# Loading the second quarter of the pole tables four rounds earlier, with PSUM split three and two instead of two and four in the first nine rounds

## Chip, cores and metric

The kernel runs on one core of a Trainium2 chip. The metric is the device time of one execution in microseconds (us); the time of a kernel is the median of several runs.

## What is computed

One transformer-like block on 2048 tokens of width 576. A modulation vector (`silu(c) @ w_mod`) gives six rows of 576. Part A is a layer norm, a modulation and a long convolution whose kernel comes from complex poles; part B is a layer norm, a modulation and a gated MLP whose gate mixes the tokens with a 2048x2048 matrix.

```python
mod = (silu(c) @ w_mod).reshape(1, 6, 1, -1)            # sa, ca, ga, sb, cb, gb
h = layernorm(x) * (1 + ca) + sa
K = einsum("dn,dnl,dn->dl", C, exp(dt*A*l), dt*B).real  # 576 channels, 128 poles, 2048 taps
x = x + ga * (irfft(rfft(h) * rfft(K)) + h * Dskip)
h = layernorm(x) * (1 + cb) + sb
z = gelu(h @ w_in); z1, z2 = halves(z)
x = x + gb * ((z1 * (w_sp @ layernorm(z2) + b_sp)) @ w_out)
```

## The kernel before

The change lies in part A, the function `ssm`. It works in **rounds** (the loop `for tick in range(NG + 4)`, L703; the first round is tick 0, so the fourth is tick 3). The 576 channels make 36 **groups** of 16, numbered g. Each round starts one group, and each group passes through a chain of steps, one round or so apart:

- `e_unit(g)` (L444), for three groups at a time in every third round: three matmuls of the table `lb` with a selector. Two fill a two-bank PSUM tile (`ps`, L450), one fills a one-bank tile (`pk`, L453). ScalarE takes the exponential of both (L451, L454).
- `t_unit(g)` (L458): matmuls of the tables `lc` and `la` (L467, L471) put the phases into a two-bank tile. For the first ten groups VectorE copies them out (L479); from group 10 on ScalarE and VectorE round them (L482, L483). L484 takes the absolute value.
- `s_unit(g)` (L487): two ScalarE sines, a cosine (L489) and a sine (L490).
- `p_unit(g)` (L492): four VectorE products (L500 to L503).
- `kg_unit(g)` (L506): 32 small matmuls into a one-bank tile (L513); ScalarE copies it to `kab` (L516), and VectorE adds the skip (L520).
- `k1_unit(g)` (L522): 8 matmuls into a one-bank tile (L530), copied out by ScalarE (L537) or VectorE (L535).

Beside this chain runs the input. In rounds 0 to 7 `ln_pair` (L423) transforms two of the 16 row blocks of x, in two halves: each half takes two two-bank tiles at once, fills them with 16 matmuls that the trace shows as 8 in bf16 and 16 in f32 (L433), and ScalarE copies each tile out (L435). The program calls a round's work LN(j) below. GpSimd then stores the block to `u_d` (L436). The row blocks come in four loads `ln_x` (L380) into two buffers, each with its statistics on VectorE (L408 to L410). In rounds 3 to 5 `mod_unit` (L342) makes one more row of the modulation: a matmul of `wm` (L349), a copy (L351), a second matmul (L354), a copy (L369 or L371) and a store by GpSimd (L372). From round 9 on `u_load`, `u_unit`, `z_unit` and `v_unit` (L572 to L603) take `u_d` through the convolution, beginning with `u_unit` (L580, L581) in round 10.

The tables `lb`, `lc` and `la` hold a quarter of the channels, nine groups, each. `poles` (L199) makes them on VectorE and ScalarE and writes them to DRAM (`pa_d`, `pb_d`) through GpSimd's queue; for the last three quarters that ends in round 2. `poles_load` (L296) brings one quarter back: a memset and six transfers of 48x1152 bf16, all issued by GpSimd in program order. Each table has two buffers. Quarter 0 is loaded ahead of the rounds, quarter 1 in round 7, quarter 2 in round 13, quarter 3 in round 21 (L787). Group 9 is the first that reads quarter 1.

PSUM has eight banks of 512 floats per partition. Through the whole of `ssm` they are two `ps` tiles of two banks and four `pk` tiles of one (L174, L182 to L186). At the start of round 9 `early.close()` (L705) ends the pools that only the input needs.

The order within an engine's queue is the program's only where the call goes through `tied` (`Pin`, L142). Most calls of the rounds don't: a scheduler sets their order when the program is built, and the wait for a PSUM tile is one of the things that it goes by. Part B is tied throughout.

Of the kernel before, what the change touches and what calls it, by code (L numbers as in the profile page):

```python
# [9 lines left out]
F32 = mybir.dt.float32  # L10
# [5 lines left out]
PSUM = bass.MemoryType.PSUM  # L16
# [148 lines left out]
def ssm(tc, I, x1_d, consts_s, dram, mod_d, mlp):  # L165
# [5 lines left out]
    with ExitStack() as ctx:  # L171
        cp = ctx.enter_context(tc.tile_pool(name="cp", reuse_waits="tile", bufs=1, side="right"))
        kp = ctx.enter_context(tc.tile_pool(name="kp", reuse_waits="tile", bufs=2, side="right"))
        psp = ctx.enter_context(tc.tile_pool(name="psp", bufs=2, space=PSUM, reuse_waits="tile"))  # L174
        early = ctx.enter_context(ExitStack())

        u1_d = dram.tile([4, 16, 2, 32, D], F32, name="u1_d")
        v_d = [dram.tile([128, 32, w], F32, name="v_d") for w in CHW]
# [1 line left out]
        pb_d = dram.tile([4, 2, 6, CW // 2], BF, name="pb_d")  # L180

        def ps2():  # L182
            return psp.tile([128, 2, 512], F32, name="ps")

        def ps1():
            return psp.tile([128, 512], F32, name="pk", bufs=4)  # L186

        mlp.ps1 = ps1
        small = cp.tile([128, 6, 128], F32, name="small")
# [106 lines left out]
        def poles_load(c, Q):  # L296
            for n, d_, k in (("lb", pb_d, 0), ("lc", pa_d, 0), ("la", pa_d, 3)):
                t_ = tb.tile([112, 9, 128], BF, name=n)
                if n == "lb":
                    Q.memset(t_[32:64], 0.0)  # L300
                for h in range(2):
                    Q.dma_start(t_[64 * h:64 * h + 48], d_[c, h, k:k + 6].rearrange("q (c g n) -> (q c) g n", c=8, g=9))
                lt[n, c] = t_
# [22 lines left out]
        def mod_load(k):  # L326

            if k < 2:
                t = kp.tile([128, 32, 128], F32, name="k1").rearrange("p a b -> p (a b)")
                wmt[k] = [t[:96, 6 * HC * hh:6 * HC * hh + 6 * HC].rearrange("p (k n) -> p k n", k=6) for hh in range(2)]  # L330
            else:
                wmt[k] = [ep.tile([96, 6, HC], F32, name="wm") for hh in range(2)]
            for hh in range(2):
                S.dma_start(wmt[k][hh], I["w_mod"][:, k, hh])
# [7 lines left out]
        def mod_unit(k):  # L342
            wm = wmt.pop(k)
            mpart = ep.tile([128, D], F32, name="mpart", bufs=1)
            pm = ps2()
            for hh in range(2):
                for kt in range(6):
                    j = kt % 4
                    T.matmul(pm[32 * j:32 * j + 32, hh, :HC], ec[:, kt:kt + 1].to_broadcast([96, 32]),  # L349
                             wm[hh][:, kt], start=kt < 4, stop=kt >= 2, skip_group_check=True)  # L350
            A.activation(v3(mpart), pm[:, :, :HC], AF.Copy)  # L351
            pm = ps2()
            for hh in range(2):
                T.matmul(pm[:, hh, :HC], ones, mpart[:, HC * hh:HC * hh + HC], start=True, stop=True)  # L354
            src = pm[:, :, :HC]
            if k == 2:
                A.activation(v3(gar), src, AF.Copy)
            elif k == 1:
                V.scalar_tensor_tensor(v3(cga), src, 1.0, v3(gar), op0=ALU.add, op1=ALU.mult)
            elif k == 0:  # L360
                V.tensor_tensor(v3(sga), src, v3(gar), op=ALU.mult)
                for i in range(2):
                    A.activation(gsp, sga, AF.Copy)
                    V.scalar_tensor_tensor(sga, gsp, msk[:, i:i + 1], sga, op0=ALU.mult, op1=ALU.add)
                A.activation(gsp, sga, AF.Copy)
            else:
                mrow = ep.tile([128, D], F32, name="gar", bufs=1)
                if k == 4:
                    A.activation(v3(mrow), src, AF.Identity, bias=one)  # L369
                else:  # L370
                    A.activation(v3(mrow), src, AF.Copy)  # L371
                G.dma_start(mod_d[k - 3:k - 2], mrow[0:1])  # L372
# [5 lines left out]
        def ln_load(i):  # L378
            x4s[i] = ep.tile([128, 4, D], F32, name="ln_x")
            S.dma_start(x4s[i], I["x"][:, 4 * i:4 * i + 4])  # L380

        def r1_load(i):
            r1t[i] = ep.tile([128, 2, 2, 32], F32, name="r1t"), ep.tile([128, 2, 2, 32], BF, name="cs")
            S.dma_start(r1t[i][0], I["c_r1t"][:, 2 * i:2 * i + 2])
            S.dma_start(r1t[i][1], I["c_cs"][:, 2 * i:2 * i + 2])
# [58 lines left out]
        def e_unit(g):  # L444
            c, gi = divmod(g, 9)
            lb = lt["lb", c]
            e = et[g] = tb.tile([128, 1536], F32, name="et", bufs=5)
            pa = ps2()
            for h, (l, r) in enumerate(zip(halves(lb, gi), rows(256, 512))):
                T.matmul(pa[:, h], l, r, start=True, stop=True)  # L450
            A.activation(e[:, :1024].rearrange("p (h n) -> p h n", h=2), pa, AF.Exp)  # L451
            pb = ps1()
            T.matmul(pb, lb[:, gi], sel[:, 1024:1536], start=True, stop=True)  # L453
            A.activation(e[:, 1024:], pb, AF.Exp)  # L454
# [113 lines left out]
        def cst_load(kg):  # L568
            cst[kg] = cs.tile([128, 8, 128], F32, name="cst%d" % kg)
            S.dma_start(cst[kg], I["c_st"][:, 8 * kg:8 * kg + 8])  # L570
# [132 lines left out]
        for tick in range(NG + 4):  # L703
            if tick == 9:
                early.close()  # L705
                cs = ctx.enter_context(tc.tile_pool(name="cs", reuse_waits="tile", bufs=1, side="right"))
                sb = ctx.enter_context(tc.tile_pool(name="sb", reuse_waits="tile", bufs=2, side="right"))
                wpre = ctx.enter_context(tc.tile_pool(name="wpre", reuse_waits="tile", bufs=2, side="right"))
            if 9 <= tick < 13:
                cst_load(tick - 9)  # L710
            if tick == 16:
                st4 = cs.tile([128, 16, 2, 64], F32, name="st4")
                S.dma_start(st4, I["c_st4"])
            if tick in (20, 24):
                mlp.start_load(tick // 4 - 5, wpre)
            todo = plan.get(tick, [])

            def go(fn):
                for f, a in todo:
                    if f is fn:  # L720
                        f(*a)

            def lag(fn, n):
                if 0 <= tick - n < NG:
                    fn(tick - n)

            if tick == 0:
                for g in range(3):
                    e_unit(g)
            go(y_load)  # L730
            go(u_load)
            es = iter(range(tick, tick + 3) if tick % 3 == 0 and 0 < tick < NG else ())

            def e_one():
                for g in es:
                    e_unit(g)
                    break

            if tick < 10:
                go(z_unit)  # L740
                lag(p_unit, 2)
                lag(t_unit, 0)
                lag(s_unit, 1)
                go(v_unit)
                lag(kg_unit, 3)
                go(u_unit)
                lag(k1_unit, 4)
                go(y_unit)
                lag(d_unit, 3)
                if tick == 0:  # L750
                    T = nc.tensor
                for _ in range(3):
                    e_one()
            else:
                go(z_unit)
                lag(p_unit, 2)
                lag(t_unit, 0)
                lag(s_unit, 1)
                lag(kg_unit, 3)
                lag(k1_unit, 4)  # L760
                go(y_unit)
                go(v_unit)
                e_one()
                go(u_unit)
                lag(d_unit, 3)
                e_one()
                e_one()
            if tick < 5:
                next(p1, None)
                next(p1, None)  # L770
            if tick == 0:
                mod_load(3)
            if 3 <= tick < 6:
                mod_unit(tick)
                if tick < 5:
                    mod_load(tick + 1)
            j = tick
            if j < 8:
                if j in (2, 4):
                    ln_stats(j // 2 + 1)  # L780
                ln_pair(2 * j)
                if j < 6:
                    r1_load(j + 2)
                if j in (1, 3):
                    ln_load(j // 2 + 2)
            if tick in (7, 13, 21):
                poles_load(1 + (tick > 7) + (tick > 13), mlp.tied.gpsimd)  # L787


        tabs.close()  # L790
# [1429 lines left out]
```

## Time and profile before

| what | us |
|---|---|
| median of 3 runs (1778.59 to 1780.67) | 1779.78 |
| the profiled execution's own time | 1784.37 |
| its span, first to last instruction | 1782.6 |
| TensorE busy, VectorE busy, ScalarE busy, GpSimd busy | 1669.4, 1259.5, 832.1, 244.5 |
| part A, rounds 3 to 9, by the copies L479 of groups 3 to 9 | 92.25 to 173.20 |
| part A, rounds 10 to 35, by L483 of groups 10 to 35 | 176.9 to 365.2 |

Times in the views are from the span's start. PE is TensorE (its matmuls), PEld its weight loads, DVE is VectorE, ACT ScalarE, POOL GpSimd, SP the queue that issues most loads. "x" stands ahead of a count. In a timeline a row has the start, the length, the engine, the line, the operation, the tile written and the tile read, and in brackets how long the engine had been idle and what ended that. L152 is a helper's line and stands for any tied call. A granted clock (PEclk) of 1.00 is TensorE's full speed.

### The profile page before, as it was taken

To read this page: it belongs to the slowest core of one execution; us is meant where nothing else is said; L and a number is where in the kernel's file an instruction comes from. 1 tells how busy PE (TensorE), PEld (TensorE's weight loads), DVE (VectorE), ACT (ScalarE), POOL (GpSimd) and SP (SyncE) were. 2 spreads that over 40 slices of the span, in tenths; PEclk is the share of its full clock that TensorE was granted. 3 is DMA by queue.
4 is the path that set the end of the run, shared out by engine and by line. 5 is a ranking of instruction groups with operands and counts; after the bars stand their busy time and mean duration, and the time that the engine had idled before them with its cause. 6 is when DMAs were issued, how large, how long until landed. Compare 5 with 4: busy or idle time off the path is not lost.

```text
span 1782.6 us, 36406 instructions
## 1 busy us (share of the span) xinstructions
PE 1669.4 (94%) x15174; PEld 1247.6 (70%) x15174; DVE 1259.5 (71%) x2259; ACT 832.1 (47%) x1118; POOL 244.5 (14%) x400
## 2 busy tenths in 40 slices
PE   3687899997899999999989999999999999999999
PEld 1243556665455445777878888888888888888887
DVE  6874899966898998688899677688344478344432
ACT  4766998844567656445434444234222223122210
POOL 3322232333122211000000000000111100111100
PEclk9587999998999999999999999999999999999999
DMA  9466646679688779767665886873767573556531
GB/s 259 134 178 184 188 121 181 184 216 294 205 255 259 248 230 266 285 245 251 233 222 165 278 302 244 269 247 124 250 219 231 195 235 98 192 195 217 193 111 40
DMA packets 183381, 376.24 MB, mean 211 GB/s; under 512 B 39360, under 2 KB 103488, under 8 KB 182448
## 3 DMA queue, kind: packets, MB, share of 16 engines
q1 hardware_dynamic: 140416, 175.23, 32.5%
q0 software_dynamic: 36896, 172.01, 29.3%
q10 hardware_dynamic: 5904, 26.67, 3.7%
q8 instruction: 119, 1.95, 0.5%
q14 instruction: 46, 0.38, 0.1%
HBM read 263.11 MB, written 101.31 MB: 204 GB/s over the span
## 4 chain that ended last, share of the span: by engine, by line
PE 65%; DVE 14%; DMA 7%; ACT 5%; issue 5%; POOL 2%; SPq 1%; ACTq 0%; DVEq 0%; POOLq 0%
PE ps L152 53%; PE pz L152 2%; DVE zset L152 2%; PE pk L513 2%; DVE bsz L152 2%; PE pk L530 2%; DMA wsst<-in_w_spT 1%; PE pk L592 1%; DVE gt L152 1%; DMA ln_x<-in_x 1%; DMA zset<-set_d 1%; PE pk L600 1%; DVE wsp L152 1%; DVE n L152 1%; DVE rq L152 1%
## 5 line engine op out<-in xcount | busy, mean ns | idle before, releaser
L152 PEld LDWEIGHTS <-zset 128*128 128x128 f16 x7182 | 702.7, 98 | 92.8 <-DVE zset L152 8.1
L152 PE MATMUL ps<-wsp,zset 128*128 128x256 f16 x6048 | 668.9, 273 | 7.1 <-DVE zset L152 6.5
L152 PE MATMUL pz<-wz,nt 128*128 128x512 f16 (+1 forms) x1120 | 224.1, 360 | 12.9 <-ACT nt L152 5.9
L152 PEld LDWEIGHTS <-nt 128*128 128x128 f16 x1120 | 109.5, 99 | 121.3 <-ACT nt L152 7.5
L152 ACT ACTIVATE z<-gt 128x1024 f16<-128x1024 f32 x56 | 59.0, 1054 | 289.6 <-DVE gt L152 289.6
L152 DVE SCALAR_TENSOR_TENSOR gt<-ps,sc,bsp 128x512 f32<-128x512 f32 x36 | 27.0, 749 | 205.0 <-PE ps L152 203.3
L1928 POOL DMA_DIRECT2D zset<-set_d x96 | 50.8, 530 | 869.7 <-PE ps L152 616.3
L152 PE MATMUL ps<-wout,z 128*128 128x288 f16 x1344 | 170.0, 286 | 0.0
L152 PEld LDWEIGHTS <-z 128*128 128x128 f16 x1344 | 131.5, 98 | 33.0
L152 DVE TENSOR_TENSOR raw<-raw 128x512 f32<-128x512 f32 (+2 forms) x228 | 119.1, 528 | 13.6 <-DMA raw<-z_d 9.3
L152 PE MATMUL ps<-n2o,zset 128*128 128x256 f16 x1134 | 128.2, 273 | 0.0
L152 DVE SCALAR_TENSOR_TENSOR gt<-ps,sc,gt 128x512 f32<-128x512 f32 (+1 forms) x180 | 122.2, 696 | 7.6
L152 DVE TENSOR_TENSOR zset<-raw,zset 128x1792 f16<-128x1792 f32 x48 | 96.9, 2019 | 14.3 <-ACT zset L152 14.3
L152 ACT ACTIVATE zset<-raw 128x1792 f16<-128x1792 f32 x48 | 81.1, 1690 | 54.7 <-PE ps L152 22.2
L152 DVE TENSOR_TENSOR z<-ps,z 128x512 f32<-128x512 f32 (+1 forms) x126 | 71.9, 598 | 36.8 <-ACT z L152 25.0
L152 ACT ACTIVATE wsp<-raw,sc 128x1792 f16<-128x1792 f32 x25 | 44.6, 1784 | 42.7 <-DVE raw L152 35.0
L152 ACT ACTIVATE z<-z,sc 128x1024 f32<-128x1024 f32 x21 | 24.1, 1148 | 75.6 <-DVE z L152 71.9
L152 ACT ACTIVATE z<-pz,sc 128x512 f32<-128x512 f32 (+1 forms) x96 | 51.7, 581 | 13.1 <-PE pz L152 7.1
L152 ACT ACTIVATE z<-z,nm,r 128x1152 f32<-128x1152 f32 x24 | 31.5, 1342 | 52.0 <-DVE nm L152 30.7
L152 PE MATMUL ps<-n2q,wf 128*128 128x512 f16 x252 | 55.7, 379 | 0.0
L501 DVE TENSOR_TENSOR pg<-et,ft 128x1024 f32<-128x1024 f32 x36 | 43.8, 1217 | 12.8 <-ACT ft L489 12.7
L152 DVE BATCH_NORM_STATS2 bsz<-z 128x6 f32<-128x384 f32 x96 | 48.4, 546 | 6.2 <-ACT z L152 5.8
(357 smaller groups left out, 2473.0 us busy)
## 6 DMA issues: line engine op xcount, KB each, us to landing
zset<-set_d POOLq DMA_DIRECT2D x96, 896.0 KB, 4.9
raw<-z_d SPq DMA_DIRECT2D x48, 512.0 KB, 5.6
set_d<-zset ACTq DMA_DIRECT2D x24, 896.0 KB, 5.9
z_d<-z POOLq DMA_DIRECT2D x32, 576.0 KB, 9.6
zset<-wa_d POOLq DMA_DIRECT2D x18, 896.0 KB, 4.9
raw<-in_w_spT SPq DMA_DIRECT2D x25, 512.0 KB, 4.3
set_d<-zset SPq DMA_DIRECT2D x12, 896.0 KB, 5.3
u_d<-st1o POOLq DMA_DIRECT2D x16, 576.0 KB, 4.2
```

Of the source, the lines that this page charges most:

```text
L152: return self.tc.keep_in_program_order(f(*a, **k))
L501: V.tensor_tensor(pr, pi, c3[:, :, None, :].to_broadcast([128, 16, 2, 32]), op=ALU.mult)
L513: T.matmul(pm[32 * j:32 * j + 32, 64 * i:64 * i + 64], x_[:, c], y_[:, c].rearrange("p s j -> p (s j)"), start=st, stop=not st, skip_group ...
L530: T.matmul(pm[64 * ri:64 * ri + 64, 128 * i:128 * i + 128], kk[:, i], r1[ri], start=True, stop=True, skip_group_check=True)
L592: T.matmul(pm[:, w * j:w * j + w], cst[k // 8][:, k % 8], k1t[c][:, k, :w], start=True, stop=True)
L600: T.matmul(pm, inva, zz[:, 0], start=True, stop=False)
L1928: self.nc.gpsimd.dma_start(o, self.set_d[f, j - 1] if j else self.wa_d[f])
```

## The change

Three things. Quarter 1 of the tables is loaded at the end of the fourth round (tick 3) in place of the eighth. The PSUM pool is opened inside `early`, with three two-bank and two one-bank tiles. At the start of round 9 that pool closes, and a new one with two and four tiles takes its place.

```diff
-        psp = ctx.enter_context(tc.tile_pool(name="psp", bufs=2, space=PSUM, reuse_waits="tile"))
         early = ctx.enter_context(ExitStack())
+        psp, wide = early.enter_context(tc.tile_pool(name="pse", bufs=2, space=PSUM, reuse_waits="tile")), 3
...
         def ps2():
-            return psp.tile([128, 2, 512], F32, name="ps")
+            return psp.tile([128, 2, 512], F32, name="ps", bufs=wide)
...
         def ps1():
-            return psp.tile([128, 512], F32, name="pk", bufs=4)
+            return psp.tile([128, 512], F32, name="pk", bufs=8 - 2 * wide)
...
             if tick == 9:
                 early.close()
+                psp, wide = ctx.enter_context(tc.tile_pool(name="psp", bufs=2, space=PSUM, reuse_waits="tile")), 2
...
-            if tick in (7, 13, 21):
-                poles_load(1 + (tick > 7) + (tick > 13), mlp.tied.gpsimd)
+            if tick in (3, 13, 21):
+                poles_load(1 + tick // 10, mlp.tied.gpsimd)
```

The number of instructions on each engine stays the same, not counting waits. Their order differs from round 0 to about round 12. In short, with E, t, KG, K1, MOD and LN for the matmuls of the steps above, a number for the group or the round, `a` and `b` for the two parts of an E (two banks, one bank), and "(9)" for a part of the 32 matmuls of a KG:

```
TensorE, from round 2, before:
 t2 LN2(half),KG0,Eb3-5 LN2(half) t3 Ea3 KG1 Ea4,5 K1.0(3) MOD3 K1.0 KG2 MOD3' LN3,K1.1 KG3(9) t4 MOD4 KG3 K1.2 MOD4' LN4,Eb6,7
 LN4,Eb8 KG4(10) t5 MOD5 KG4 K1.3 MOD5' LN5(half) KG5(15) LN5 KG5(15) t6 Ea6 KG5,K1.4 Ea7,8 LN6 t7 LN7(8) KG6 LN7 KG6 t8 K1.5 E9-11,KG7,t9 ...
TensorE, from round 2, changed:
 t2 LN2(4) KG0(4) Eb3 KG0 Eb4 LN2(2) Eb5 LN2 t3 Ea3-5 MOD3 KG1(25) MOD3' LN3 t4 KG1 K1.0 MOD4 KG2 MOD4' LN4 t5 K1.1
 MOD5 KG3(17) MOD5' LN5 t6 KG3 K1.2 Ea6 Eb6 Ea7 Eb7 Ea8 LN6(3) Eb8 LN6 t7 KG4 K1.3 LN7 t8 KG5 K1.4 t9 KG6 K1.5 E9-11 ...
VectorE, changed: ... L479(2), statistics of ln_x 2 with the pole work between, rt of LN2, p1, p2, L479(3), ... L479(4), half of p3,
 statistics of ln_x 3, rest of p3, p4 with L418, L479(5), L479(6), p5, L479(7), p6, L479(8), p7, L479(9), p8, ...
ScalarE, changed, end of the stretch: ... sin8, kab, cos9, k, exp table, e9-e11, L482(10), sine table, sin9, kab, k, uu, L482(11), cos10, sin10, kab, k, uu, L482(12)
GpSimd, changed: ... store of mod row 3, two stores of LN3, memset and six loads of quarter 1, store of mod row 4, two stores of LN4, ...
```

On SP two loads change places with a neighbour; nothing else differs in part A.

## Prediction

> **What bounds the kernel now.** The page's chain of work that ended last has TensorE on most of the program, but the changed lines work only in its first tenth. So the view to start from is a set of stretches, with the busy time of PE, PEld, DVE, ACT and POOL, the granted clock, the DMA share and GB/s.
>
> ```profile
> 60.00:100.00 40.00, 29.46 (x337) 13.49 (x340) 37.10 (x91) 29.47 (x43) 16.22 (x24) 0.57 0.51 153
> 100.00:157.30 57.30, 47.70 (x771) 25.78 (x759) 35.74 (x73) 37.84 (x55) 10.22 (x14) 0.85 0.55 175
> 157.30:173.20 15.90, 8.27 (x90) 4.07 (x89) 4.61 (x8) 7.76 (x10) 3.37 (x7) 0.57 0.93 252
> 173.20:189.30 16.10, 11.24 (x194) 8.27 (x194) 13.80 (x18) 14.20 (x17) 2.23 (x4) 0.81 0.85 258
> 189.30:365.20 175.90, 165.11 (x2422) 102.35 (x2421) 160.31 (x201) 161.26 (x215) 52.99 (x92) 1.00 0.55 157
> ```
>
> There are three regimes. From 60 to 100 us VectorE is busy 37.10 of 40 us: it bounds. From 189 us on, three engines are all over 91%: a balanced pipe, which can't catch up or lose much. Between them no engine is full, and from 157.3 to 173.2 none is busy much more than half the time. The next view, the chain in order of time, says why.
>
> ```profile
> 156.30 1.09 POOL lb L152
> 157.67 0.77 POOL lb L152
> 158.44 7.02 DMA lb<-pb_d
> ```
>
> The load of quarter 1 stands in GpSimd's queue behind the last store of the input, so its memset begins at 156.30, and the first table is whole at 165.5 (158.44 + 7.02). VectorE waits with it:
>
> ```profile
> 156.40 1.22 DVE L479 COPY ft<-ps 128x1024 f32<-128x1024 f32 x1
> ...
> 160.70 1.22 DVE L500 TENSOR_TENSOR pg<-et,ft 128x1024 f32<-128x1024 f32 x1
> 161.84 0.68 DVE L502 SCALAR_TENSOR_TENSOR et<-ft,et 128x512 f32<-128x512 f32 x1
> ...
> 173.20 1.23 DVE L479 COPY ft<-ps 128x1024 f32<-128x1024 f32 x1 [10.08 <-PE ps L467]
> L483 DVE SCALAR_TENSOR_TENSOR ft<-ft,ps x26: 1208/1211/1222, 176.9 to 365.2; 128x1024 f32<-128x1024 f32 x26
> ```
>
> Group 9's copy comes 16.8 us after group 8's; later a round takes (365.2 - 176.9) / 25 = 7.53 us.
>
> **The early load.** The DRAM copy that it reads is written by the end of round 2, so it is free to move. In the changed program it stands in GpSimd's queue behind the stores of LN3 and ahead of that of modulation row 4. Of before, first the gap in question, then the last issue of the load in its old place:
>
> ```profile
> 107.44 0.76 POOL L436 DMA_DIRECT2D u_d<-st1o  x1 [1.44 <-ACT st1o L435]
> 113.91 0.53 POOL L372 DMA_DIRECT2D mod_d<-gar  x1 [5.71 <-ACT gar L369]
> ...
> 159.96 1.00 POOL L152 DMA_DIRECT2D la<-pa_d  x2
> ```
>
> Memset and six issues took 156.30 to 160.96 in the old place, 4.7 us; the gap between 108.2 and 113.9 holds 5.7. So GpSimd delays nobody, and if it did, only a 2 KB store would wait. Where it was taken away GpSimd has nothing to do before the `uu` transfers of round 10.
>
> What it saves I work out on ScalarE, which sets the pace of rounds 8 to 12. Its rows of before:
>
> ```profile
> 159.43 1.04 ACT L490 ACTIVATE ft<-ft 128x1024 f32<-128x1024 f32 x1
> 160.49 1.28 ACT L451 ACT_TABLE_LOAD   x1
> ...
> 180.19 1.09 ACT L482 ACTIVATE ft<-ps,consts_s 128x1024 f32<-128x1024 f32 x1
> 181.18 1.14 ACT L489 ACTIVATE ft<-ft,consts_s 128x1024 f32<-128x1024 f32 x1
> 182.22 1.04 ACT L490 ACTIVATE ft<-ft 128x1024 f32<-128x1024 f32 x1
> 183.17 0.36 ACT L516 ACTIVATE kab<-pk 128x256 f32<-128x256 f32 x1
> 183.43 0.59 ACT L537 ACTIVATE k<-pk 128x512 f32<-128x512 f32 x1
> 183.91 0.60 ACT L581 ACTIVATE uu<-pk 128x512 f32<-128x512 f32 x1
> 184.38 1.13 ACT L482 ACTIVATE ft<-ps,consts_s 128x1024 f32<-128x1024 f32 x1
> ...
> 191.87 1.03 ACT L451 ACTIVATE et<-ps 128x1024 f32<-128x1024 f32 x1
> 192.79 0.59 ACT L454 ACTIVATE et<-pk 128x512 f32<-128x512 f32 x1
> ```
>
> From the end of group 8's sine (160.47) to group 12's rounding (184.38) it takes 23.9 us. From start to start, L482 costs 0.99, a cosine 1.04, a sine 0.95, `kab` 0.26, k 0.48, `uu` 0.47, an exponential pair 0.92 + 0.48 = 1.40, a table load 1.28. The changed order between the same points: `kab` 0.26; group 9's cosine, 1.04, ahead of it a wait of 2.4 (VectorE needs some 5.1 us from group 8's absolute value to group 9's, two products of 1.22, two of 0.68, a copy and the absolute value, 0.1 of each overlapped; ScalarE's cosine, k and sine of group 8 cover 2.5 and `kab` 0.2); k 0.48; table 1.28; three pairs 4.2; L482 0.99; table 1.28; sine 0.95; `kab`, k, `uu` 1.21; L482 0.99; cosine, sine 1.99; `kab`, k, `uu` 1.21. That is 18.3 us, **5.6 us saved**. Behind it nothing is late: the last input store moves with LN7, and what it gates, `u_unit`, comes two rounds behind.
>
> The bounds. Taking the whole stall off, 16.8 - 7.5 = 9.3. If TensorE's low clock stays in the new order, its matmuls hold ScalarE up: 8.27 us of them at 0.57 would be 4.7 at full clock, so 3.6 could come back, and 2.0 is left. The Trainium skill, "TensorE: Matmul & The Clock Gate", "What's actually happening", says that the clock halves after an idle window of about 3.4 us and needs as long a busy one to return; the trace agrees, with a wait of 7.02 us and 0.57 granted around it, and by that rule the end to expect without the wait is the upper one, 9.3, rather than 2.0.
>
> **The new transfers' company.** They now run beside the last load of x, which VectorE waits for:
>
> ```profile
> 105.00:115.10 10.10, 9.71 (x172) 5.68 (x171) 2.36 (x5) 5.80 (x9) 2.08 (x3) 1.00 0.83 265
> 115.09 1.18 DVE L408 BATCH_NORM_STATS2 bs<-ln_x 128x6 f32<-128x288 f32 x3 [5.30 <-DMA ln_x<-in_x]
> lb<-pb_d POOLq DMA_DIRECT2D x4, 108.0 KB, 4.6
> ```
>
> Six times 108 KB is 0.65 MB, at 265 GB/s 2.4 us. The new ones start from 108, when the load of x is on its way: between 0 and 2.4 us, I take 1, the smaller half, as a part of x has come by then. The Trainium skill, "DMA: Bandwidth & Descriptors", "Issuing engines are not separate DMA queues", says that transfers from any engine interleave on the same 16 DMA engines; that speaks for the upper end, and the sum would be 1.4 us less of a gain.
>
> **Three two-bank tiles.** TensorE's waits for PSUM, in total us, times and longest, from 40 to 160 us:
>
> ```profile
> PE ps L433 <- ACT st1o L435: 11.5, 8, 4.3
> PE ps L433 <- DVE ft L479: 2.7, 2, 1.7
> ```
>
> The top of what it can bring is their sum, 14 us. But while VectorE bounds, up to 100 us, no such wait is worth anything; I put rounds 0 to 3 at nothing. In round 2 it could even cost: VectorE's changed order sets the scales `rt` of LN2 behind the statistics of x: eight at 1.18 for three, 3.1 us, with six pole products between them and two waits for ScalarE, some 9 us in all by an estimate.
>
> From the landing of the last x on I walk the changed order. Copy L479 of group 5 has as much VectorE work ahead of it behind the landing as before, so it stays. LN5 may begin at that copy, as a third tile is free, where it waited for the sine and the modulation row; its copies come 2 to 3 us sooner. In round 6 ScalarE spends them again: exponentials, table load, four copies; cosine 6 stays. Group 7 gets its phases before LN7 takes its tiles and without waiting for exponentials: the walk has cosines 7 and 8 at 146 and 153.5, of before:
>
> ```profile
> 151.18 1.15 ACT L489 ACTIVATE ft<-ft,consts_s 128x1024 f32<-128x1024 f32 x1 [0.41 <-DVE ft L484]
> ...
> 158.38 1.15 ACT L489 ACTIVATE ft<-ft,consts_s 128x1024 f32<-128x1024 f32 x1 [0.43 <-DVE ft L484]
> ```
>
> So sine 8 is some 4.7 us early. The walk gives every matmul TensorE's full clock, whereas 0.85 was granted from 100 to 157; I take **3.4 us**, with 0 and 7 (half of the sum of waits) as ends.
>
> **One-bank tiles.** Two for four: KG and K1 of one group take turns, each freed by ScalarE's copy, which the next step needs anyway. The three Eb of a round want a third tile and make TensorE wait for an exponential in rounds 3, 6 and 9; the walk holds those waits. Opening the pool anew in round 9 costs nothing, as the tiles under it were read before.
>
> **Sum.** 5.6 + 3.4, the company being in the walk: 9 us less. Behind 189 us the balanced pipe hands it on, and the later parts, whose loads wait for buffers freed by work, start earlier by as much. The profiled execution's own 1784.4 becomes 1775.4. That run stands 4.6 us above the median of the runs shown, so against the median it is 1779.8 - 9.0 = **1770.8 us**.
>
> **Rivals.**
>
> *Early rounds slip (slower).* Place: rounds 2 and 3. LN2 waits for `rt`, and Eb5, which stands inside LN2 in TensorE's queue, for an exponential; LN3 behind them frees the buffer of the last x, and all to the end of round 8 goes by its landing. For it: the 9 us above. Against: VectorE has 37.10 of 40 us of work there in either order, so LN2 and LN3 had little to gain from an early `rt`. It decides once the landing slips by more than 5.6 us, from 115.1 to 120.7. With the full 9 and 1.4 for shared transfers, 9 + 1.4 - 5.6 = 4.8 slower: 1784.6 us.
>
> *The split is neutral.* Only the load counts: 1779.8 - 5.6 = 1774.2 us. For it: ScalarE loads its tables as often as before and spends round 6's gain.
>
> *The stall was hidden.* Something later sets the end of part A, such as the loads and stores after round 35, or the early load moves the wait to the `u` loads behind LN7. For it: the store ahead of the memset at 156.30 gates `u_d` too. Against: the balanced pipe from 189 us, in which no queue waits long. 1779.8 us.
>
> *A warm TensorE.* At full clock the 8.27 us at 0.57 and 11.24 at 0.81 would be 4.7 and 9.1, 5.7 us less; half of it on the path is 3 more: 1767.8 us. The clock rule named above is on its side, and the waits that stay are against it.
>
> **How the numbers follow.** Forecast 0.36, neutral split 0.2, warm 0.14, hidden 0.14, slip 0.16. A change under 0.2%, 3.6 us, is about what a measurement can't tell from none. Faster: forecast, neutral, warm less a little for their edges, 0.69; within: 0.15; slower: 0.16. For 8 times in 10 the range goes from the sum of the upper ends, 9.3 + 7 = 16.3 (1763.5), to part of the slip, 1783.0. The forecast's own range is 1765 to 1776.
>
> **What would show it.** Right: in the changed trace GpSimd's memset near 108 us, no wait of L450 for `lb`, copies of groups 8 and 9 under 8 us apart, L482 of group 12 near 175.5 instead of 184.38, and the same 7.5 us a round after. LN5 begins within 2 us of copy 5. Wrong: the statistics of the last x later than 118 us; a wait of KG or Eb for a one-bank tile of several us; a longer round after 189; or a lead at 189 us that is gone by 440.

## The result and the profile after

The changed kernel takes 1771.31 us (median of 12 runs, 1769.23 to 1776.38) where the kernel before, run beside it, takes 1779.29 (12 runs, 1775.77 to 1781.11). The ratio is 0.9961, with a 95% interval of 0.9949 to 0.9974: by the ratio 6.9 us faster (4.6 to 9.1), by the medians 8.0. Forecast were 1770.8 us, 9 less than before. The sum is near; its terms are not all so, as the experiments show.

The profiled execution of the changed kernel took 1773.69 us, with a span of 1771.9. First the stretches of the changed kernel, cut at its own copies of groups 8 and 9 (columns as in the prediction; the 1.00 of the first row is not full speed, see the last section):

```profile
60.00:100.00 40.00, 23.11 (x231) 10.46 (x229) 36.15 (x89) 26.44 (x35) 15.88 (x24) 1.00 0.49 152
100.00:154.80 54.80, 44.25 (x751) 24.92 (x747) 31.55 (x65) 37.47 (x53) 13.29 (x20) 0.84 0.62 186
154.80:159.50 4.70, 4.70 (x123) 3.34 (x111) 4.63 (x7) 3.24 (x5) 0.50 (x1) 1.00 0.95 296
159.50:183.80 24.30, 18.18 (x276) 11.02 (x276) 17.62 (x24) 22.23 (x29) 2.15 (x4) 0.77 0.93 291
183.80:357.40 173.60, 164.34 (x2412) 101.52 (x2412) 160.18 (x201) 158.43 (x212) 52.73 (x91) 0.99 0.56 157
```

The stall of 15.9 us has become a stretch of 4.7, in which VectorE is busy 4.63. ScalarE then carries the stretch to group 12 (22.23 of 24.30). Behind it the balanced pipe is as it was. The timelines of GpSimd, VectorE and ScalarE in the changed kernel, and its row of L483:

```profile
108.70 1.08 POOL L152 MEMSET lb<- 32x1152 bf16 x1
...
112.11 0.99 POOL L152 DMA_DIRECT2D la<-pa_d  x2
114.47 0.50 POOL L372 DMA_DIRECT2D mod_d<-gar  x1 [1.36 <-ACT gar L369]
```
```profile
153.96 1.22 DVE L479 COPY ft<-ps 128x1024 f32<-128x1024 f32 x1 [1.11 <-PE ps L467]
...
159.50 1.22 DVE L479 COPY ft<-ps 128x1024 f32<-128x1024 f32 x1
L483 DVE SCALAR_TENSOR_TENSOR ft<-ft,ps x26: 1207/1212/1222, 169.8 to 357.4; 128x1024 f32<-128x1024 f32 x26
```
```profile
157.48 1.05 ACT L490 ACTIVATE ft<-ft 128x1024 f32<-128x1024 f32 x1
...
161.48 1.15 ACT L489 ACTIVATE ft<-ft,consts_s 128x1024 f32<-128x1024 f32 x1 [2.68 <-DVE ft L484]
...
168.65 1.11 ACT L482 ACTIVATE ft<-ps,consts_s 128x1024 f32<-128x1024 f32 x1
...
177.45 1.16 ACT L482 ACTIVATE ft<-ps,consts_s 128x1024 f32<-128x1024 f32 x1
```

The load's memset begins at 108.70 in place of 156.30, and the modulation store behind it hardly moves (114.47; 113.91 before). The copies of groups 8 and 9 stand 5.5 us apart (16.8 before), and a round behind takes (357.4 - 169.8) / 25 = 7.50 us. L482 of group 12 comes at 177.45 in place of 184.38.

But positions in two traces can't be subtracted as they stand. Up to its first scale `rt` (L420) the input's work is the same in both kernels, and already there the traces differ. Of before, and then of the changed kernel:

```profile
40.76 0.25 DVE L420 TENSOR_SCALAR rt<-r1t,r 128x64 f32<-128x64 f32 x1 [0.79 <-DMA r1t<-in_c_r1t]
...
92.25 1.21 DVE L479 COPY ft<-ps 128x1024 f32<-128x1024 f32 x1
...
204.95 1.21 DVE L483 SCALAR_TENSOR_TENSOR ft<-ft,ps 128x1024 f32<-128x1024 f32 x1
```
```profile
38.52 0.25 DVE L420 TENSOR_SCALAR rt<-r1t,r 128x64 f32<-128x64 f32 x1 [1.35 <-DMA r1t<-in_c_r1t]
...
94.38 1.22 DVE L479 COPY ft<-ps 128x1024 f32<-128x1024 f32 x1
...
116.54 1.18 DVE L408 BATCH_NORM_STATS2 bs<-ln_x 128x6 f32<-128x288 f32 x3 [5.07 <-DMA ln_x<-in_x]
...
197.19 1.22 DVE L483 SCALAR_TENSOR_TENSOR ft<-ft,ps 128x1024 f32<-128x1024 f32 x1
```

The first scale comes at 40.76 and at 38.52, and in the eleven profiles below between 38.64 and 40.22, whatever the split of PSUM: 2.24 us of the lead is the start of these two executions. So this table counts from the first scale; each ratio is to runs of before on the same chip. It holds the copy L479 of group 3, the statistics L408 of the last x, the start of sine 8 (L490), and L483 of group 14, from where the lead stays the same to group 35 (204.95 - 197.19 and 365.20 - 357.44 are both 7.76).

| us from the first scale | copy 3 | last x | sine 8 | L483 of g14 | median, us | ratio to before, 95% |
|---|---|---|---|---|---|---|
| before | 51.49 | 74.33 | 118.67 | 164.19 | 1779.29 | |
| changed | 55.86 | 78.02 | 118.96 | 158.67 | 1771.31 | 0.9961 (0.9949 to 0.9974) |
| 1 load alone | 51.43 | 72.33 | 117.51 | 153.23 | 1766.76 | 0.9934 (0.9919 to 0.9950) |
| 2 split alone | 55.88 | 77.43 | 120.19 | 163.96 | 1777.57 | 0.9998 (0.9987 to 1.0008) |
| 3 load in round 5 | 53.41 | 73.69 | 113.73 | 153.18 | 1769.21 | 0.9945 (0.9925 to 0.9966) |
| 4 both pairs first | 49.82 | 70.10 | 109.24 | 148.86 | 1759.85 | 0.9891 (0.9876 to 0.9907) |
| 5 as 4, no split | 51.49 | 74.73 | 120.06 | 155.77 | 1767.87 | 0.9941 (0.9921 to 0.9961) |
| 6 as 4, back in round 8 | 48.27 | 68.92 | 107.09 | 144.36 | 1755.82 | 0.9882 (0.9861 to 0.9903) |
| 7 split in rounds 4 to 7 | 51.30 | 73.79 | 119.83 | 156.78 | 1768.90 | 0.9951 (0.9933 to 0.9969) |
| 8 as 6, load in round 5 | 49.60 | 68.08 | 106.08 | 143.63 | 1756.50 | 0.9889 (0.9869 to 0.9908) |
| 9 pair of round 2 first | 49.35 | 68.49 | 106.79 | 146.41 | 1758.54 | 0.9876 (0.9859 to 0.9893) |
| 10 pair of round 4 first | 56.18 | 77.99 | 118.18 | 157.13 | 1769.59 | 0.9935 (0.9918 to 0.9951) |
| 11 back in round 8 | 53.52 | 76.49 | 119.02 | 155.26 | 1767.01 | 0.9923 (0.9910 to 0.9937) |

Read by stretches, the changed kernel loses 3.7 us to the last x (78.02 - 74.33), gains 3.4 from there to sine 8 (44.34 becomes 40.94) and 5.8 from sine 8 to group 14 (45.52 becomes 39.71): 5.5 us in all. The measured 6.9 to 8.0 contain up to 2.5 us more. Behind group 14 these two executions differ by 2.9 us more (1577.6 us to the end in before, 1574.7 in the changed kernel), but the split alone, which gains nothing, has 1574.8 there too, so the rest can't be put down to a cause (each profile is one execution).

What went wrong in the early rounds stands in the waits. Of the changed kernel, VectorE's timeline, then TensorE's:

```profile
79.45 0.46 DVE L408 BATCH_NORM_STATS2 bs<-ln_x 128x6 f32<-128x288 f32 x1 [2.71 <-DMA ln_x<-in_x]
...
85.55 0.20 DVE L420 TENSOR_SCALAR rt<-r1t,r 128x64 f32<-128x64 f32 x1
...
106.30 0.74 DVE L420 TENSOR_SCALAR rt<-r1t,r 128x64 f32<-128x64 f32 x2 [6.32 <-PE ps L433]
```
```profile
85.81 0.76 PE L433 MATMUL ps<-ln_x,rt 32*64 32x288 f32 x4 [9.13 <-DVE rt L420]
```

In the changed order the scale of LN2 stands behind the statistics of the third x, and these first wait for that x to land. So the scale comes at 85.55 (76.69 before), TensorE stands 9.13 us in the middle of LN2, and VectorE itself waits 6.32 us for LN3 at 106.3.

### The profile page after: what moved, and what is told of

Read it like the earlier page. It is cut to its first block, busy times and chain, and to the rows that moved or that the text cites. A ratio compares the mean times of both kernels' runs of the same rounds, so it can differ in the third digit from the quotient of the medians.

```text
span 1771.9 us, 36402 instructions
## 1 busy us (share of the span) xinstructions
PE 1664.0 (94%) x15174; PEld 1244.7 (70%) x15174; DVE 1259.0 (71%) x2259; ACT 831.6 (47%) x1118; POOL 245.2 (14%) x400
## 5 line engine op out<-in xcount | busy, mean ns | idle before, releaser
L152 PE MATMUL pz<-wz,nt 128*128 128x512 f16 (+1 forms) x1120 | 222.5, 358 | 12.8 <-ACT nt L152 5.6
L152 PE MATMUL ps<-wout,z1b 128*128 128x288 f16 x384 | 52.4, 286 | 0.0
L152 DVE SCALAR_TENSOR_TENSOR wsp<-raw,sc,wsp 128x1792 f16<-128x1792 f32 x25 | 51.9, 2078 | 0.0
```

What stands on the lines that cost most here:

```text
L152: return self.tc.keep_in_program_order(f(*a, **k))
```

## The experiments

**1. The load alone.** Before, with one line changed; PSUM stays two and four.

```diff
-            if tick in (7, 13, 21):
-                poles_load(1 + (tick > 7) + (tick > 13), mlp.tied.gpsimd)
+            if tick in (3, 13, 21):
+                poles_load(1 + tick // 10, mlp.tied.gpsimd)
```

> Before, with the load of quarter 1 in round 3 and PSUM split as before. Theory (the early load brings most of the 8.0 us, since it ends the wait of group 9 for its table): the copy of group 9 comes under 9 us after that of group 8 instead of 16.8, L482 of group 12 some 5 us earlier than 184.38, the constant lead behind group 14 some 5 us, and the time 4.5 to 6 us less than before (ratio 0.9966 to 0.9975). Rival (the split carries it, and the end of the wait only brings the next one forward): the copy of group 9 is near, but the lead behind group 14 is under 2 us and the time within 2 us of before.

Measured: 1766.76 us, ratio 0.9934, 11.7 us faster: about twice the theory's 4.5 to 6, and 4.5 us below the whole change (the two intervals just touch; experiment 5, a second kernel with the load and no split, has 0.9941). ScalarE's timeline of this run:

```profile
156.37 1.04 ACT L490 ACTIVATE ft<-ft 128x1024 f32<-128x1024 f32 x1
...
159.21 1.02 ACT L451 ACTIVATE et<-ps 128x1024 f32<-128x1024 f32 x1
...
165.85 1.15 ACT L489 ACTIVATE ft<-ft,consts_s 128x1024 f32<-128x1024 f32 x1
...
173.84 1.11 ACT L482 ACTIVATE ft<-ps,consts_s 128x1024 f32<-128x1024 f32 x1
```

Here the exponentials of groups 9 to 11 (from 159.21) stand ahead of cosine 9, which therefore waits for nothing. From sine 8 to L482 of group 12 it takes 17.5 us; in the changed kernel, with cosine 9 first and its wait of 2.68, 20.0 (177.45 - 157.48). To L483 of group 14 the load alone saves 45.52 - 35.72 = 9.8 us, and in the changed kernel 5.8.

**2. The split alone.** The changed kernel, with the load back in round 7 (the lines of experiment 1 the other way round).

> The changed kernel with the load of quarter 1 back in round 7, so that only the split of PSUM stands against before. Theory (sine 8 comes 1.9 us earlier by the split in the trace of the changed kernel, but the memset stands behind the last store of the input, which moved by 1.0 us only): the memset of the load at 154 to 156 instead of 156.30, the wait of group 9 stays at 9 us or more, and the time is 0.5 to 2.5 us less than before. Rival (the forecast's 3.4 us is a gain of its own): 3.4 us less, with a lead of 3 us or more behind group 14. Second rival (the split has nothing to bring): within 0.5 us.

Measured: 1777.57 us, ratio 0.9998 (0.9987 to 1.0008): nothing, or at most 2.3 us. A gain of 3.4 is excluded; between the theory's lower part and the second rival the run does not decide. The memset came at 157.21, not earlier than before, and the copies of groups 8 and 9 stand 15.8 us apart. Copy 3 and the last x are as late as in the changed kernel (55.88 and 77.43), so that lateness comes with the split, not with the load.

**3. The load in round 5.** The changed kernel with `if tick in (5, 13, 21):`.

> The changed kernel with the load of quarter 1 at the end of round 5 instead of round 3, so that it no longer runs beside the last load of x. Theory (that company costs the 1.45 us by which the statistics of the last x came later, and the path goes over them): the statistics of the last x are back at 115.1, within 0.4, group 9 still has its table in time, and L482 of group 12 comes 0.7 to 1.5 us earlier than 177.45, with as much off the time. Rival (the path from 100 to 157 us goes over the modulation weights that TensorE waited 5.3 us for, or the statistics are late because of the late scales of LN2 and LN3 and not of the company): the statistics may come earlier or not, and L482 of group 12 stays within 0.5 us.

Measured: 1769.21 us, ratio 0.9945 (0.9925 to 0.9966), 2.1 us below the changed kernel by medians, within the intervals of both. The last x does come earlier (73.69 against 78.02 from the first scale), but copy 3 is 2.45 us earlier already, at 93.27, long before either kernel loads quarter 1. So this run could not price the company; experiment 8 does. Copy 3 comes at 55.9 to 56.2 in three of the kernels with the late scales of LN2 and at 53.4 to 53.5 in two (this one and the eleventh), with the same early order on VectorE in all five. The statistics of the third x, which stand ahead of the scale of LN2, begin 40.9 to 41.3 us from the first scale in the three and 38.3 to 38.6 in the two, and VectorE waited 2.6 to 3.0 us for that x in the three and at most 0.4 in the two: the difference comes with the landing of that load.

**4. LN pairs ahead of the statistics.** The changed kernel, with the pair of rounds 2 and 4 built first:

```diff
+                ln_pair(2 * j)
                 if j in (2, 4):
                     ln_stats(j // 2 + 1)
-                ln_pair(2 * j)
```

> The changed kernel with LN pairs 2 and 4 built ahead of the statistics that stand ahead of them (rounds 2 and 4), so that the scales of LN2 don't stand behind the statistics of the next x on VectorE. Theory (VectorE bounds rounds 0 to 3 in either order, so TensorE's 9.1 us wait for the scales of LN2 costs nothing by itself): the scales of LN2 come near 77 as before the change, TensorE's wait is gone, but the copy of group 4 and L482 of group 12 stay within 1 us and the time within 1.5 us of the changed kernel. Rival (that wait is what the split of PSUM lost of the forecast's 3.4 us): L482 of group 12 1.5 us or more earlier than 177.45, and as much off the time.

Measured: 1759.85 us, ratio 0.9891, 11.5 us below the changed kernel by medians. The theory falls, and with it the forecast's reason for setting the early rounds at nothing; the rival was right in kind, and too small.

**5. The same without the split.** Experiment 1 with the pairs of experiment 4.

> Load of quarter 1 in round 3, PSUM split as before, and LN pairs 2 and 4 ahead of the statistics as in the fourth experiment. Theory (the other place of the pairs only mends what the split had put late, the scales of LN2 behind the statistics of the next x; without the split they are in time anyway): within 2 us of the early load alone, 1765 to 1769 us, and L479 of group 3 comes 51.4 us behind the first scale of the trace's window (38.86 with the early load alone), within 0.6. Rival (the place of the pairs is a gain of its own): 4 us or more below the early load alone, down to the 1759.9 of the fourth experiment, so that the split brings nothing.

Measured: 1767.87 us, ratio 0.9941; copy 3 at 51.49. As the theory had it: without the split, the place of the pairs is worth nothing. So it mends a lateness that the split brought, and with the split it does more than mend: in experiments 4, 6, 8 and 9 the last x has its statistics 68.1 to 70.1 us from the first scale, where before has 74.33 and the load alone 72.33. Between this run and the sixth, which both have the load and the pairs, the split, with its end in round 8, is worth 12.1 us by medians, 10.5 by the ratios.

**6. Two and four again from round 8.** Experiment 4, with the PSUM pool on a stack of its own (here called `pse`):

```diff
-            if tick == 9:
-                early.close()
-                psp, wide = ctx.enter_context(...), 2
+            if tick == 8:
+                pse.close()
+                psp, wide = ctx.enter_context(...), 2
+            if tick == 9:
+                early.close()
```

> The fourth experiment with PSUM opened anew as two and four at the start of round 8 instead of round 9. In the built order ScalarE then has the exponentials of groups 9 to 11 ahead of the cosine of group 9, as with the early load alone. Theory (the cosine of group 9 ahead of the exponentials, with its 2.7 us wait for VectorE and the longer way from sine 8 to L482 of group 12, is what the change lost behind round 8: 18.9 us against 16.4 with the early load alone): from the end of sine 8 to L482 of group 12 at most 17 us instead of 18.9, the wait of cosine 9 under 1 us, and the time 2.5 to 4.5 us less than the 1759.9 us of the fourth experiment. Rival (the longer way only reflects where the two kernels stand when they come there): within 1 us of the fourth experiment.

Measured: 1755.82 us, ratio 0.9882; 4.0 us below the fourth by medians, 1.6 by the ratios, and the intervals overlap. In the trace the wait of cosine 9 is gone, and sine 8 to L483 of group 14 takes 37.3 us in place of 39.6. To L482 of group 12 it takes 18.6 from start to start, 17.5 from the end of sine 8 (17 at most were expected; the changed kernel's 18.9). This is the fastest of the kernels by its median.

**7. The split in rounds 4 to 7 only.** The changed kernel, two and four in rounds 0 to 3 and, by the edit of experiment 6, again from round 8; statistics and pairs as they were.

```diff
+            if tick == 4:
+                pse.close()
+                psp, wide = pse.enter_context(...), 3
```

> The changed kernel with three and two tiles in rounds 4 to 7 only, two and four before and after; statistics and pairs in their old order. Theory (the split loses in rounds 2 and 3, where it puts the scales of LN2 late, gains 3 to 5 us between the landing of the last x and sine 8, and loses again behind round 8): TensorE's 9.1 us wait for the scales of LN2 is gone, from the statistics of the last x to the end of sine 8 it takes 40 to 43 us instead of the 46.2 with the early load alone, and the time is 2.5 to 5 us less than the early load alone, 1762 to 1764.5 us. Rival (the split gains nothing in the middle, and only the changed order of the early rounds shortened what comes behind): within 1.5 us of the early load alone, 1766.8.

Measured: 1768.90 us, ratio 0.9951: not below the load alone, as the rival said. The reason is not the rival's. VectorE's and ScalarE's timelines of this run (line numbers are one higher here):

```profile
124.00 1.22 DVE L480 COPY ft<-ps 128x1024 f32<-128x1024 f32 x1
...
155.65 1.22 DVE L480 COPY ft<-ps 128x1024 f32<-128x1024 f32 x1 [1.15 <-PE ps L468]
```
```profile
146.94 1.15 ACT L490 ACTIVATE ft<-ft,consts_s 128x1024 f32<-128x1024 f32 x1
```

From cosine 6 to copy 8 it takes 8.7 us, as with the split everywhere (8.5 to 8.7 in eight others, 9.6 in the eleventh), where two and four take 12.8 to 13.3. So the middle does gain its 4 us. But from copy 5 to cosine 6 it takes 22.9 us, 18.0 to 19.7 in all others. Why opening the pool in round 4 makes that stretch 3 to 5 us longer stays open.

**8. The company of the loads.** Experiment 6 with the load in round 5 (`tick in (5, 13, 21)`).

> The sixth experiment with the load of quarter 1 at the end of round 5 instead of round 3, to price its company with the last load of x in an order that is otherwise the same. Theory (1 us as forecast, 0 to 2.4 by the bytes): from the issue of the last x's load to the statistics of it 0.5 to 1.5 us less, and as much off the time, at most 2.4. Rival (the 2.4 us by which the third experiment's time lies below that of the changed kernel were mostly the earlier landing of the x before it, and the company costs nothing): issue to statistics within 0.3 us, and the time within 1 us.

Measured: 1756.50 us, ratio 0.9889: the same as the sixth within 1 us. Issue of the last x on SP's queue and its statistics, in the sixth run:

```profile
101.32 0.38 SPq L381 DMA_DIRECT2D ln_x<-in_x  x1
...
108.39 1.18 DVE L409 BATCH_NORM_STATS2 bs<-ln_x 128x6 f32<-128x288 f32 x3 [1.06 <-DMA ln_x<-in_x]
```

and in the eighth:

```profile
100.54 0.38 SPq L381 DMA_DIRECT2D ln_x<-in_x  x1
...
108.07 1.17 DVE L409 BATCH_NORM_STATS2 bs<-ln_x 128x6 f32<-128x288 f32 x3
```

7.07 us with the company, 7.53 without. In the eighth VectorE no longer waits for the x, so the second number holds some of VectorE's own lateness; from issue to landing alone the profiles have 7.0 and 7.2 us. Over all profiles the way from issue to statistics is 6.9 to 10.6 us in the nine kernels with the load in round 3, and 7.5 to 9.1 in the four without. Company costs nothing that these show, against a scatter of some 2 us; the rival was right.

**9. The pair of round 2 alone.** As the fourth, for `j == 2` only.

> The changed kernel with LN pair 4 (that of LN2) alone ahead of the statistics, in round 2; round 4 as in the changed kernel. All positions are told from the first scale of the trace. Theory (the late scales of LN2 are what the split costs in the early rounds): TensorE's 9.1 us wait is gone, the copy of group 3 comes 49.8 us behind the first scale as in the fourth experiment instead of 55.9, the statistics of the last x 5 to 8 us earlier than the 78.0 of the changed kernel, and the time 5 to 8 us less than the 1771.3 of the changed kernel, 1763.5 to 1766.5. Rival (the pair of round 4 carried the gain of the fourth experiment): less than 3 us off the time, though the copy of group 3 comes early.

Measured: 1758.54 us, ratio 0.9876: the whole gain of the fourth experiment, and more than the theory's 5 to 8. Of this run VectorE's and TensorE's timelines, and its windows beside those of the changed kernel:

```profile
39.62 0.26 DVE L420 TENSOR_SCALAR rt<-r1t,r 128x64 f32<-128x64 f32 x1 [1.67 <-DMA r1t<-in_c_r1t]
...
77.91 0.24 DVE L420 TENSOR_SCALAR rt<-r1t,r 128x64 f32<-128x64 f32 x1
...
88.97 1.22 DVE L479 COPY ft<-ps 128x1024 f32<-128x1024 f32 x1
...
108.11 1.18 DVE L408 BATCH_NORM_STATS2 bs<-ln_x 128x6 f32<-128x288 f32 x3 [0.58 <-DMA ln_x<-in_x]
```
```profile
78.20 0.76 PE L433 MATMUL ps<-ln_x,rt 32*64 32x288 f32 x4 [0.41 <-DVE rt L420]
```
```profile
60.00:100.00 40.00, 31.91 (x367) 16.05 (x365) 38.02 (x92) 33.74 (x46) 16.98 (x26) 1.00 0.61 185
100.00:118.00 18.00, 12.78 (x208) 6.73 (x206) 16.17 (x38) 7.71 (x12) 8.02 (x12) 0.94 0.97 299
```

Of the changed kernel, the second of these stretches (the first stands above):

```profile
100.00:118.00 18.00, 16.29 (x310) 9.79 (x306) 6.36 (x12) 14.01 (x21) 7.57 (x13) 1.00 0.87 258
```

TensorE's wait of 9.13 us is 0.41. From 60 to 100 us VectorE is busy 38.02 and 36.15 us, hardly different. The cost shows behind that: from 100 to 118 us it finds 16.17 us of work here and 6.36 in the changed kernel, where it stands waiting for LN3 and the last x (6.32 and 5.07). From 60 to 100 us TensorE does 31.91 us of work here, and 23.11 in the changed kernel. The edit is this one place, but the scheduler built more than that anew: the rest of KG1 and K1.0 (L530 at 94.71) stand ahead of LN3, and behind t4 in the changed kernel (107.55). So the 12.8 us are shown for the order that comes of this place, not for the wait of 9.13 us by itself.

**10. The pair of round 4 alone.** As the fourth, for `j == 4` only.

> The changed kernel with LN pair 8 (that of LN4) alone ahead of the statistics, in round 4; round 2 as in the changed kernel. Theory (the pair of round 4 shortens only the way from the statistics of the last x to the copy of group 5, 7.4 us in the fourth experiment against 10.0): the copy of group 3 stays at 55.9 us behind the first scale, the statistics of the last x at 78.0 within 1.5, the way to the copy of group 5 is 7.4 us, and the time 1.5 to 3.5 us less than the 1771.3 of the changed kernel. Rival (TensorE's modulation weights or the table loads set round 6, so that a copy that is early there brings nothing): within 1 us of the changed kernel.

Measured: 1769.59 us, ratio 0.9935 (0.9918 to 0.9951), 1.7 us below the changed kernel by medians, within the intervals. Copy 3 and the last x stay late (56.18 and 77.99) as expected, but the way from the statistics to copy 5 is 9.96 us and not 7.4. The theory's mechanism falls: the 7.4 us of the fourth run belong to the pair of round 2 (7.40 in the ninth).

**11. Back in round 8, alone.** The changed kernel with the edit of experiment 6.

> The changed kernel with PSUM opened anew as two and four at the start of round 8 instead of round 9, nothing else. Theory (the order that the changed kernel has at group 9 costs 2.4 us from sine 8 to the sum L483 of group 14, by the sixth experiment against the fourth, and the start alone with the early load up to 4.0): the way from the start of sine 8 to the first L483 of group 14 is 36 to 38 us instead of 39.7, and the time 2 to 4 us less than the 1771.3 of the changed kernel. Rival (where nothing is early in front of it, the order at group 9 makes no difference): within 1 us of the changed kernel.

Measured: 1767.01 us, ratio 0.9923 (0.9910 to 0.9937), 4.3 us below the changed kernel by medians. From sine 8 to L483 of group 14 it takes 36.2 us in place of 39.7. The order at group 9 does cost 3.5 us; copy 3 came 2.3 us earlier in this run as well, as in the third, but by sine 8 nothing of that is left (119.02 against 118.96).

## Why the prediction came near, and which steps failed

**The stall and the early load: right in mechanism and, for this kernel, in size.** The walk had 5.6 us with a wait of 2.4 for cosine 9. Measured are 5.8 to group 14 (5.0 to group 12), with a wait of 2.68. What the prediction did not see is that the walk already held a cost of the split. It took the changed order as the order of the load. With PSUM as before the same load saves 9.8 us, just over the "9.3" given as upper end: of the 4 us between, 2.5 lie up to L482 of group 12, where cosine 9 stands ahead of the exponentials and waits, and the rest behind it. The prediction had that end come with a faster TensorE clock: the granted clock was 0.77 there in the changed kernel, from 159.5 to 183.8, and 0.92 in the load alone, from 155.2 to 177.3. The clock does not make the difference. Experiment 9 has the changed kernel's order at group 9 and a higher clock; from sine 8 to L482 of group 12, of the changed kernel and then of experiment 9:

```profile
157.48:177.45 19.97, 15.87 (x241) 9.37 (x231) 15.97 (x20) 17.23 (x24) 1.11 (x2) 0.74 0.88 287
```
```profile
146.41:166.38 19.97, 12.90 (x240) 7.07 (x230) 15.98 (x21) 17.23 (x25) 1.11 (x2) 0.93 0.93 295
```

TensorE's work shrinks by 3 us and the stretch stays at 19.97; to group 14 it takes 39.71 and 39.62. So with this order the rival "a warm TensorE" brings nothing here, and its 3 us fall away.

**"Opening the pool anew in round 9 costs nothing": failed.** TensorE has no wait of several us for an old tile there, as was argued. The cost came with the order: built with the opening in round 9, cosine 9 stands ahead of the exponentials, and built with it in round 8, behind them. That gave 2.3 to 3.5 us back from sine 8 to group 14 (experiments 6 and 11).

**The split in the middle: right in kind, and the figure is partly luck.** The walk gave 4.7 us (4.9 by its cosine 8, 158.38 - 153.5), 3.4 were taken. From the statistics of the last x to sine 8 the changed kernel gains 3.4, but the four other kernels with the late scales of LN2 gain between 1.6 and 4.3 there. From cosine 6 to copy 8 every kernel with the split gains 3 to 5 us on two and four.

**"I put rounds 0 to 3 at nothing": failed, and it is the step that mattered most.** The split costs 4.4 us by copy 3 and 3.7 by the last x, which eats the 3.4 of the middle: before and the changed kernel reach sine 8 within 0.3 us of each other. The rival "early rounds slip" had the place and the cause, `rt` of LN2 behind the statistics, at a price of 9 us against a margin of 5.6. It was set aside with the reason that VectorE is full there in either order. That reason does not hold. VectorE was as full (36.15 of 40 us), but with work that was not the next needed, and behind it little was ready, 6.36 us of work from 100 to 118 against 16.17 in experiment 9. It went wrong in a second way: the statistics were priced at their own time, while the first of them waits in VectorE's queue for a load to land. Experiment 9, whose edit is this place alone, gains 12.8 us by medians (15 by the ratios). The nothing was wrong in the other direction too: of these 12.8 us only some 4 take back the lateness; with the scales in time, the split brings the last x to 68.49 us from the first scale, where the three kernels on two and four have 72.33 to 74.73.

**The company: taken at 1 us in the walk, measured at nothing** (7.0 against 7.2 us from issue to landing). The Trainium skill, "DMA: Bandwidth & Descriptors", "Issuing engines are not separate DMA queues", has transfers from different engines run on the same 16 DMA engines and interleave. Nothing here speaks against that. But 0.65 MB beside the 1.15 MB of the last x did not delay it by an amount that shows.

So the sum of 9 came within 1 to 2 us of the result with one term (3.4) that was eaten elsewhere, and that it came so near is in part luck: the traces hold 5.5 us of the measured 6.9 to 8.0, and what makes up the rest is open. As built, the split brings nothing (0.9998 alone; sine 8 within 0.3 us; beside the load it even costs 4.5 us by medians), as the rival "the split is neutral" had it, though not for its reason. "The stall was hidden" is out by the load alone.

Of the signs named in advance, the memset, the copies, the length of a round and the constant lead came true. L482 of group 12 came at 177.45 and not near 175.5. The one for a slip ("later than 118 us") missed it by the start: 116.54 is 118.8 on the clock of before. Cosines 7 and 8 came at 148.95 and 155.95, on the clock of before 4.7 to 5.2 us behind the walk, 3.7 of it with the last x; LN5's first matmuls came at 131.0, 4.5 us behind copy 5 and not 2.

## What to carry to other kernels

A busy engine does not excuse a late instruction in its queue: ask what the work put ahead of it waits for, above all a load, and which engine stands idle behind it. Where a scheduler builds the order, a change of buffers moves instructions far from the buffers; read the new order at each place that it moves, and price a change by its parts, since one good part can hide a bad one (here both pieces of the loss could be taken back, for 1755.8 us in place of 1771.3). Count positions in two traces from an event that both share.

## What the runs showed that was not expected

The start is not the same from execution to execution: the first scale, with the same input work ahead of it, lies between 38.52 and 40.76 us in thirteen profiles, and each time a transfer ended the idle time before it.

A granted clock of 1.00 in a profile need not be full speed. Around TensorE's long wait in the changed kernel the windows show:

```profile
76.00:86.00 10.00, 0.87 (x11) 0.30 (x13) 7.29 (x25) 4.20 (x5) 2.56 (x5) 1.00 0.38 117
```

That reads as if the clock had not fallen in a stretch in which TensorE is busy 0.87 of 10 us. But the matmuls themselves tell otherwise. TensorE's timeline of the changed kernel, ahead of the wait, behind it and later, and then two rows of before:

```profile
69.01 0.61 PE L471 MATMUL ps<-sel 48*128 48x512 bf16 x2
...
89.47 0.61 PE L471 MATMUL ps<-sel 48*128 48x512 bf16 x2
...
133.84 0.39 PE L471 MATMUL ps<-sel 48*128 48x512 bf16 x2
```
```profile
74.76 0.61 PE L471 MATMUL ps<-sel 48*128 48x512 bf16 x2
...
136.00 0.39 PE L471 MATMUL ps<-sel 48*128 48x512 bf16 x2 [0.29 <-ACT st1o L435]
```

In before a pair of these matmuls takes 0.61 us where 0.50 is granted (72 to 76 us), and 0.39 where 1.00 is (136 to 140). The changed kernel shows 1.00 at all three of its rows, yet two of them take 0.61: by the matmuls TensorE ran slow ahead of the wait and behind it, and the 1.00 shown there can't be full speed. The same holds early in the profile of experiment 9 (0.61 at 84.41, with 1.00 shown). The Trainium skill, "TensorE: Matmul & The Clock Gate", "What's actually happening", has the clock halve after an idle window of about 3.4 us. This wait can neither confirm nor refute that, since the matmuls were as slow ahead of it. So a granted clock is best read beside the length of a matmul whose form recurs.
